# Sink attention and an erf-softplus feed-forward layer on one core: weight blocks held, converted and split two at a time

## The chip, the cores and the metric

The kernel runs on one core of a Trainium2 chip. The metric is the device time of one launch in microseconds (us). A profile of one execution comes with it. In the profile PE is TensorE (matmuls), PEld its weight loads, DVE VectorE, ACT ScalarE, POOL GpSimd, and SP the engine whose queue issues nearly all DMAs.

## The reference

Inputs are `q`, `k`, `v` of shape 4 x 8 x 768 x 64 (batch, heads, positions, head size), float32, and two weight matrices in float64: `w_in` 512 x 2048 and `w_out` 2048 x 512.

```python
keep = (pos[None, :] < n_sink) | ((rel >= 0) & (rel < window))      # n_sink 4, window 128
scores = where(keep, q @ k.T / sqrt(D), -1e9)
a = softmax(scores);  attn = a @ v                                   # -> x: 3072 tokens x 512
h = x @ w_in
g = h * erf(softplus(h))
out = g @ w_out                                                      # float32
```

## The kernel before

**Work.** Tokens are handled in 12 groups of 256. A group needs four attention steps (two heads each; `s` counts them over the whole kernel, 48 in all), and then 16 slices `f` of 128 hidden columns. `m` = 16 x group + f counts slices. Two slices share one PSUM tile `h`, of which there are two; `act` turns a tile into `g` with three ACT squares in a row, three more into a ring `u`, and three DVE passes (line 635), the first of which reads `h` and so frees its tile. `project` multiplies `g` by `w_out` and adds into `o`.

**Two kinds of product.** From group 1 on each float32 value is a pair of rounded parts, high and low, and a product takes three matmuls (lines 616 and 656 to 658). Group 0 uses the plain float32 weights `wf` (lines 612 and 653), since the pairs are not made yet. The profile counts each such float32 matmul twice.

**Weights.** There are 32 blocks of 128 x 512: 16 of `w_in`, 16 of `w_out`. `wload` brings a block in as raw 64-bit words (512 KB), `wconv` makes float32 of it on DVE in three passes (lines 513, 517, 523), the last few with an ACT copy behind (530), and `wsplit` makes the pair: an ACT cast for the high part (536), a DVE subtraction for the low part (537). Raw words, float32 blocks and pairs share one pool of 33 tiles of 4 KB a partition. The passes of `wconv` work in tiles of the ring `u`, which has three buffers and belongs to `act` as well.

**An attention step** is: `prep` (transposes of q and k on PE, a copy to `kq` on ACT), `score` (PE into `ps`; DVE masks at 343 and 348; ACT exponentials at 352), `norm` (DVE, for steps 4 to 7 ACT too), `ptrans` (PE transposes 383 and 384; ACT copies `pa` and `pz`; POOL selections at 397) and `av` (PE, line 424). `core(s)` is `av(s - 2)` followed by `score(s)`. `xh` and `xl` (442, 443) are the pair of a step's result; slice 0 of group 1 needs those of steps 4 to 7.

**Order.** Every engine works its own queue strictly in order. The order is not written by hand: each piece gets a priority from its step `a` = m + 10 and a table of offsets, and a scheduler that simulates the program places instructions by it. A change of sizes can therefore move instructions on every engine.

Of the kernel before, what the change touches and what calls it, by code (L numbers as in the profile page):

```python
# [19 lines left out]
P = 128  # L20
# [16 lines left out]
W1 = 7  # L37
WQ = 5
# [14 lines left out]
def kernel(  # L53
# [27 lines left out]
    wpool = ctx.enter_context(tc.tile_pool(name="wpool", bufs=33))  # L81
# [49 lines left out]
    def fast_path():  # L131
        with ExitStack() as st:
# [107 lines left out]
            def first_v():  # L240

                t = first_tile("v")
# [242 lines left out]
            staged = {}  # L485
# [3 lines left out]
            order = sorted(range(32), key=need)  # L489
            split = {}  # L490
            for n in range(32):
                split.setdefault(NF - 5 + n // 4 * 4 + n % 4 if n < 16 else NF + n - 16 + 1, []).append(n)

            def wload(n):

                src = wblock(n)
                t = staged[n] = wpool.tile([P, 2 * DM], I32, tag="wo", name=f"ws_{n}")
                if src.dtype == F32:
                    nc.sync.dma_start(t[:, :DM].bitcast(F32), src)
                else:  # L500
                    nc.sync.dma_start(t, src.bitcast(I32))

            def wconv(n, wn):

                s = staged.pop(n)
                if wblock(n).dtype == F32:
                    t = s[:, :512].bitcast(F32)
                else:
# [14 lines left out]
                    nc.vector.scalar_tensor_tensor(  # L523
                        out=ti if late else wf[n].bitcast(I32), in0=w[:, :, 0], scalar=29, in1=ti,
                        op0=ALU.logical_shift_right, op1=ALU.bitwise_or,
                    )
                    if not late:
                        return
# [282 lines left out]
```

## Time and profile before

| | us |
|---|---|
| median of 3 runs (763.35 to 765.52) | 763.46 |
| the profiled execution, as timed | 763.33 |
| span of its trace | 761.6 |
| PE busy / ACT / DVE / POOL | 720.0 / 549.0 / 494.2 / 231.9 |

The timed execution is 1.7 us longer than the span of its trace. A busy PE is not PE at its peak: its granted clock falls to half after pauses, and this is shown beside the stretches. The page's slices show PE below nine tenths only in roughly the first fifth of the span and at the very end.

### The profile page before, as it was taken

Reading aid. Unit: us, or ns where it says so; the run is one execution under the profiler, and the core shown is the slowest. Engines: PE = TensorE matmul, PEld = TensorE weight load, DVE = VectorE, ACT = ScalarE, POOL = GpSimd, SP = SyncE. Lnnn points to the kernel's source line nnn. Section 1 sums busy time; section 2 is a strip of 40 time slices with the busy share of each in tenths; the row PEclk is TensorE's granted clock in tenths of the full one; section 3 lists DMA queues with packets and bytes.
Section 4 is the critical chain, followed back from the end, with each engine's and each line's share of the span. In section 5 each row is a group of like instructions: output and inputs, shape, how many; then the busy total and the mean of one; then the engine's idle time right before and its main releaser. Section 6 shows DMA issues by size and latency. Waiting matters only on the chain. (4 is left out here: it accounts for less than half of the span.)

```text
span 761.6 us, 16545 instructions
## 1 busy us (share of the span) xinstructions
PE 720.0 (95%) x5840; PEld 612.9 (80%) x5840; DVE 494.2 (65%) x1383; ACT 549.0 (72%) x1293; POOL 231.9 (30%) x289
## 2 busy tenths in 40 slices
PE   4678998799999999999999999999999999999997
PEld 3456575688898898898898898888888888889895
DVE  5999977886565575576476475485476476475352
ACT  3446696987886786787687687687687687696574
POOL 0352211224224234233333333333332332332222
PEclk9688999999999999999999999999999999999999
DMA  8987512211311321221212222212222221110000
GB/s 229 234 273 262 166 36 49 75 32 34 85 44 35 83 51 32 71 46 42 72 43 50 77 45 44 64 41 52 60 49 53 53 63 43 43 46 2 28 2 32
DMA packets 115963, 54.13 MB, mean 71 GB/s; under 512 B 93153, under 2 KB 108513, under 8 KB 115873
## 3 DMA queue, kind: packets, MB, share of 16 engines
q1 hardware_dynamic: 114944, 52.86, 26.3%
q8 instruction: 49, 0.80, 0.5%
q14 instruction: 42, 0.34, 0.1%
q10 hardware_dynamic: 928, 0.13, 0.1%
HBM read 38.28 MB, written 6.29 MB: 59 GB/s over the span
## 5 line engine op out<-in xcount | busy, mean ns | idle before, releaser
L616 PE MATMUL h<-xh,wt 128*128 128x256 f32 x1408 | 273.5, 284 | 5.6 <-DVE acc L635 5.6
L616 PEld LDWEIGHTS h<-xh,wt 128*128 128x128 f32 x1408 | 224.4, 189 | 14.0 <-DVE acc L635 8.3
L616 PE MATMUL h<-xl,wt 128*128 128x256 f32 x704 | 198.4, 282 | 0.0
L641 POOL TENSOR_TENSOR g<-acc,g 128x512 fp32r<-128x512 f32 x88 | 114.1, 1297 | 272.8 <-DVE g L640 228.5
L633 ACT ACTIVATE u<-r 128x512 f32<-128x512 f32 x288 | 163.7, 622 | 14.7 <-DVE wf L523 7.1
L635 DVE SCALAR_TENSOR_TENSOR acc<-u,h 128x512 f32<-128x512 f32 x88 | 60.4, 686 | 140.1 <-POOL g L641 70.4
L656 PE MATMUL o<-wt,g 128*128 128x512 f32 x352 | 141.7, 402 | 0.0
L397 POOL TENSOR_SCALAR_AFFINE_SELECT pz<-pa 64x256 f32<-64x256 f32 x96 | 67.3, 701 | 243.0 <-ACT pa L387 239.9
L657 PE MATMUL o<-wt,g 128*128 128x512 f32 x352 | 139.4, 396 | 0.0
L616 PEld LDWEIGHTS h<-xl,wt 128*128 128x128 f32 x704 | 132.9, 189 | 4.6 <-issue 0.5
L635 DVE SCALAR_TENSOR_TENSOR acc<-u,acc 128x512 f32<-128x512 f32 x176 | 124.7, 709 | 17.8 <-DVE acc L635 0.9
L658 PE MATMUL o<-wt,g 128*128 128x512 f32 x352 | 135.4, 397 | 0.0
L352 ACT ACTIVATE pst<-pst,neg 128x144 f32<-128x144 f32 x192 | 77.4, 404 | 32.6 <-DVE neg L348 31.7
L658 PEld LDWEIGHTS o<-wt,g 128*128 128x128 f32 x352 | 65.8, 187 | 14.9 <-POOLq L779 0.5
L628 ACT ACTIVATE r<-h 128x512 f32<-128x512 f32 x96 | 56.9, 592 | 26.4 <-PE h L616 23.9
L657 PEld LDWEIGHTS o<-wt,g 128*128 128x128 f32 x352 | 66.1, 188 | 11.7
L656 PEld LDWEIGHTS o<-wt,g 128*128 128x128 f32 x352 | 66.1, 188 | 11.5 <-ACT ot L662 0.4
L630 ACT ACTIVATE r<-r 128x512 f32<-128x512 f32 x96 | 60.7, 632 | 2.7
L629 ACT ACTIVATE r<-r 128x512 f32<-128x512 f32 x96 | 60.9, 635 | 2.0
L442 ACT CAST xh<-av 128x256 fp32r<-128x256 f32 x44 | 16.0, 365 | 53.1 <-PE av L424 53.1
L367 DVE TENSOR_SCALAR pst<-pst,sum 128x128 f32<-128x128 f32 x176 | 50.5, 350 | 1.5
L286 ACT COPY kq<-tqk 128x512 f32<-128x512 f32 x48 | 28.0, 585 | 32.6 <-PE tqk L283 28.3
(86 smaller groups left out, 933.5 us busy)
## 6 DMA issues: line engine op xcount, KB each, us to landing
ws<-in_moe_w_in_dram SPq DMA_DIRECT2D x16, 512.0 KB, 5.1
ws<-in_moe_w_out_dram SPq DMA_DIRECT2D x16, 512.0 KB, 5.7
v<-in_v_dram SPq DMA_DIRECT2D x64, 96.0 KB, 2.3
out_dram<-ot SPq DMA_DIRECT2D x24, 256.0 KB, 2.1
q<-in_q_dram SPq DMA_DIRECT2D x88, 64.0 KB, 2.2
k<-in_k_dram SPq DMA_DIRECT2D x88, 64.0 KB, 2.1
vz<-v SPq DMA_DIRECT2D x88, 64.0 KB, 2.1
kq<-kq SPq DMA_DIRECT2D x32, 64.0 KB, 2.0
```

Of the source, the lines that this page charges most:

```text
L352: nc.scalar.activation(y, y, AF.Exp, bias=d["neg"][:, i, h : h + 1], scale=-1.0, accum_out=d["sum"][:, i, h : h + 1])
L397: nc.gpsimd.affine_select(out=out, in_=x, pattern=[[0, 2], [0, 2], [-sg, HP]], compare_op=op, fill=0.0, base=0, channel_multiplier=sg,)
L616: nc.tensor.matmul(o, wt[NC * j + c][:, p, fs], xt[e][:, c, :], start=(m == 0), stop=(m == len(ops) - 1))
L628: nc.scalar.activation(r, h, AF.Tanh, bias=b_t, scale=0.5)
L629: nc.scalar.activation(r, r, AF.Square, bias=b_v, scale=-0.5)
L630: nc.scalar.activation(r, r, AF.Square, bias=b_r)
L633: nc.scalar.activation(u, r, AF.Square, bias=b_a[i], scale=CS)
L635: nc.vector.scalar_tensor_tensor(out=acc, in0=u, scalar=CC[i] * CS**2, in1=x, op0=ALU.add, op1=ALU.mult)
L641: nc.gpsimd.tensor_tensor(gl, acc, gh.bitcast(F32), op=ALU.subtract)
L656: nc.tensor.matmul(o, gh[:, ws], wt[16 + f][:, 0, :], start=(f == 0), stop=False)
L657: nc.tensor.matmul(o, gh[:, ws], wt[16 + f][:, 1, :], start=False, stop=False)
L658: nc.tensor.matmul(o, gl[:, ws], wt[16 + f][:, 0, :], start=False, stop=(f == NF - 1))
```

## The change

Blocks go two to a tile. `wload` brings 1 MB in one DMA; `wconv` makes its three DVE passes over 1024 words, in place in the tile `wf`, with no ring `u` and no ACT copy; each conversion's first pass is told to follow the last pass of the conversion before. `wsplit` casts and subtracts 1024 words. High parts live in tiles of four blocks, in a ring of eight 8 KB tiles that the raw pairs use too; low parts and float32 pairs share 17 tiles of 4 KB. First `q`, `k` and `v` tiles lie in the ring of eight.

```diff
-WQ = 5
+WQ = 3
-    wpool = ctx.enter_context(tc.tile_pool(name="wpool", bufs=33))
+    wpool = ctx.enter_context(tc.tile_pool(name="wpool", bufs=17))
+    hpool = ctx.enter_context(tc.tile_pool(name="hpool", bufs=8))
...
-            order = sorted(range(32), key=need)
+            order = sorted(range(0, 32, 2), key=need)
...
-                t = staged[n] = wpool.tile([P, 2 * DM], I32, tag="wo", name=f"ws_{n}")
+                t = staged[n] = hpool.tile([P, 2, 2 * DM], I32, tag="big", name=f"ws_{n}")
...
-                    nc.sync.dma_start(t, src.bitcast(I32))
+                    nc.sync.dma_start(t, src.bitcast(I32).rearrange("(i p) d -> p i d", p=P))
...
-                    t = work.tile([P, 512], F32, tag="u", bufs=UB, name=f"w_{n}")
-                    w = s.rearrange("p (n t) -> p n t", t=2)
-                    ti = t.bitcast(I32)
...
-                    late = wn >= 33 - WQ
-                    if not late:
-                        wf[n] = wpool.tile([P, 2 * DM], F32, tag="wo", name=f"wf_{n}")[:, :DM]
...
-                wf[n] = wpool.tile([P, 2 * DM], F32, tag="wo", name=f"wf_{n}")[:, :DM]
-                nc.scalar.copy(wf[n], t)
+                d = wpool.tile([P, 2, DM], F32, tag="wf", name=f"wf_{n}")
+                w = s.rearrange("p i (n t) -> p (i n) t", t=2)
+                ti = d.rearrange("p i n -> p (i n)").bitcast(I32)
+                first = nc.vector.tensor_scalar(
+                    ti, w[:, :, 1], 0x07FFFFFF, 3, op0=ALU.bitwise_and, op1=ALU.logical_shift_left
+                )
+                follow(mark.get("c"), first)
...
+                mark["c"] = nc.vector.scalar_tensor_tensor(
+                    out=ti, in0=w[:, :, 0], scalar=29, in1=ti, op0=ALU.logical_shift_right, op1=ALU.bitwise_or
+                )
...
             def wsplit(n):
 
-                t = wf.pop(n)
-                d = wt[n] = wpool.tile([P, 2, DM], F32R, tag="wo", name=f"wt_{n}")
-                nc.scalar.copy(d[:, 0, :], t)
-                nc.vector.tensor_tensor(d[:, 1, :], t, d[:, 0, :].bitcast(F32), op=ALU.subtract)
+                d = wp.pop(n)
+                if n % 4 == 0:
+                    hq[n // 4] = hpool.tile([P, 4, DM], F32R, tag="big", name=f"wh_{n}")
+                hi_ = hq[n // 4][:, n % 4 : n % 4 + 2]
+                lo_ = wpool.tile([P, 2, DM], F32R, tag="wf", name=f"wl_{n}")
+                nc.scalar.copy(hi_, d)
+                nc.vector.tensor_tensor(lo_, d, hi_.bitcast(F32), op=ALU.subtract)
```

What the scheduler makes of it is seen in the order of instructions. Lines 612, 616, 635, 653 of before are 606, 610, 629, 647 of the change; 513, 517, 523 are 515, 520, 523; 536 and 537 are 535 and 536. In a name the first number is the step, slice or block, the last a running number.

Place 1, DVE, around the first pass of the first `act` (`gf_1`, slices 0 and 1). Before, from the conversion of blocks 10 and 11 on:

```order
L513 TENSOR_SCALAR w_11_686<-ws_11_606 128x512
L517 SCALAR_TENSOR_TENSOR w_10_679<-ws_10_599,w_10_679 128x512
L523 SCALAR_TENSOR_TENSOR wf_9_655<-ws_9_592,w_9_652 128x512
L517 SCALAR_TENSOR_TENSOR w_11_686<-ws_11_606,w_11_686 128x512
L523 SCALAR_TENSOR_TENSOR wf_10_682<-ws_10_599,w_10_679 128x512
L343 COPY_PREDICATED ps_5_617<-tri_134,ps_5_617 64x2x2x64
L523 SCALAR_TENSOR_TENSOR wf_11_689<-ws_11_606,w_11_686 128x512
L635 SCALAR_TENSOR_TENSOR gf_1_716<-u0_1_720,h_0_659 128x512
```

With the change the same pass stands here:

```order
L515 TENSOR_SCALAR wf_18_559<-ws_18_497 128x1024
L520 SCALAR_TENSOR_TENSOR wf_18_559<-ws_18_497,wf_18_559 128x1024
L523 SCALAR_TENSOR_TENSOR wf_18_559<-ws_18_497,wf_18_559 128x1024
L515 TENSOR_SCALAR wf_8_595<-ws_8_532 128x1024
L629 SCALAR_TENSOR_TENSOR gf_1_650<-u0_1_654,h_0_601 128x512
L520 SCALAR_TENSOR_TENSOR wf_8_595<-ws_8_532,wf_8_595 128x1024
```

Sixteen blocks are converted ahead of it before; with the change twelve, and the first pass of two more.

Place 2, DVE, the masks of attention step 7 (`ps_7`). Before, the first three splits of the kernel (`wt_0`, `wt_1`, `wt_2`) lie around them, and `gf_11` comes later:

```order
L537 TENSOR_TENSOR wt_0_1175<-wf_0_325,wt_0_1175 128x512
L443 TENSOR_TENSOR xl_1_845<-av_5_956,xh_1_844 128x256
L343 COPY_PREDICATED ps_7_973<-tri_134,ps_7_973 64x2x2x64
L635 SCALAR_TENSOR_TENSOR gf_9_1090<-u2_9_1100,gf_9_1090 128x512
L537 TENSOR_TENSOR wt_1_1201<-wf_1_332,wt_1_1201 128x512
L343 COPY_PREDICATED ps_7_973<-tri_134,ps_7_973 64x2x2x64
L348 ISA pst_142,neg_7_972<-ps_7_973,mask_84 128x144
```

With the change:

```order
L536 TENSOR_TENSOR wl_10_1472<-wf_10_621,wh_8_1373 128x1024
L629 SCALAR_TENSOR_TENSOR gf_15_1172<-u2_15_1182,gf_15_1172 128x512
L443 TENSOR_TENSOR xl_1_755<-av_5_842,xh_1_754 128x256
L536 TENSOR_TENSOR wl_20_1476<-wf_20_663,wh_20_1475 128x1024
L343 COPY_PREDICATED ps_7_859<-tri_137,ps_7_859 64x2x2x64
L536 TENSOR_TENSOR wl_12_1587<-wf_12_743,wh_12_1586 128x1024
L343 COPY_PREDICATED ps_7_859<-tri_137,ps_7_859 64x2x2x64
L536 TENSOR_TENSOR wl_22_1590<-wf_22_674,wh_20_1475 128x1024
L348 ISA pst_145,neg_7_858<-ps_7_859,mask_87 128x144
```

There are now eleven of the sixteen pair splits, and all eight `act` of group 0, ahead of the masks of step 7; the last five splits follow directly.

Place 3, PE, around `core(7)`, that is `av_5` and the scores of step 7. Before, it stands between the projection of `gf_7` and the hidden slices 12 and 13 of group 0:

```order
L653 MATMUL o_0_1_864<-wf_23_758,gf_7_1004 128x512
L424 MATMUL av_5_956<-pa_5_704,v_5_502 64x64 x2
L424 MATMUL av_5_956<-pa_5_704,v_5_502 64x128 x2
L424 MATMUL av_5_956<-pa_5_704,v_5_502 64x64 x2
L424 MATMUL av_5_956<-pz_5_705,vz_139 64x64 x8
L331 MATMUL ps_7_973<-kq_137 64x208 x2
L331 MATMUL ps_7_973<-kq_137 64x224 x2
L331 MATMUL ps_7_973<-kq_137 64x208 x2
L331 MATMUL ps_7_973<-kq_137 64x224 x2
L283 MATMUL tqk_8_1045<-ident_61,k_8_998 128x128 x2
L283 MATMUL tqk_8_1045<-ident_61,q_8_995 128x128 x2
L612 MATMUL h_12_1178<-xf_0_424,wf_12_828 128x256
```

With the change:

```order
L647 MATMUL o_0_1_774<-wf_28_903,gf_13_1097 128x512
L424 MATMUL av_5_842<-pa_5_638,v_5_484 64x64 x2
L424 MATMUL av_5_842<-pa_5_638,v_5_484 64x128 x2
L424 MATMUL av_5_842<-pa_5_638,v_5_484 64x64 x2
L424 MATMUL av_5_842<-pz_5_639,vz_142 64x64 x8
L331 MATMUL ps_7_859<-kq_140 64x208 x2
L331 MATMUL ps_7_859<-kq_140 64x224 x2
L331 MATMUL ps_7_859<-kq_140 64x208 x2
L331 MATMUL ps_7_859<-kq_140 64x224 x2
L283 MATMUL tqk_8_923<-ident_64,k_8_884 128x128 x2
```

Group 0 has done all its hidden slices and seven of its eight projections by then. What follows is one projection, nine matmuls of group 1, and the transposes of step 7.

## Rows read from the trace of the kernel before

**Rows 1.** Busy time of each engine in stretches of the span (us from its start), each with its number of instructions; then the granted PE clock as a share of full speed, the DMA share and GB/s.

```profile
20.00:30.00 10.00, 5.22 (x37) 4.42 (x37) 9.80 (x41) 4.79 (x18) 2.15 (x4) 0.55 0.88 176
50.00:60.00 10.00, 4.47 (x35) 3.21 (x34) 8.77 (x17) 4.99 (x10) 5.62 (x4) 0.93 0.92 315
60.00:70.00 10.00, 10.00 (x28) 6.86 (x29) 9.94 (x28) 6.30 (x18) 0.00 (x0) 0.73 0.99 367
90.00:100.00 10.00, 10.00 (x78) 6.89 (x77) 9.80 (x18) 8.43 (x17) 3.74 (x4) 1.00 0.12 29
120.00:130.00 10.00, 7.19 (x57) 4.93 (x59) 6.21 (x23) 6.59 (x18) 2.04 (x4) 0.84 0.18 40
140.00:150.00 10.00, 7.49 (x48) 6.92 (x47) 8.77 (x25) 9.91 (x25) 2.02 (x2) 0.87 0.39 105
200.00:300.00 100.00, 99.61 (x859) 87.75 (x858) 63.45 (x185) 78.06 (x185) 33.38 (x43) 1.00 0.23 57
```

**Rows 2.** PE in order of time: start, duration, line, operation, out<-in, count, and in brackets the idle time before with what ended it.

```profile
59.95 6.37 PE L612 MATMUL h<-xf,wf 128*128 128x256 f32 x16 [5.53 <-DVE gf L635]
...
70.14 3.62 PE L612 MATMUL h<-xf,wf 128*128 128x256 f32 x16
...
127.00 1.12 PE L424 MATMUL av<-pa,v 128*64 128x64 f32 x12 [2.81 <-issue]
...
143.67 0.39 PE L656 MATMUL o<-wt,g 128*128 128x512 f32 x1
143.90 0.40 PE L657 MATMUL o<-wt,g 128*128 128x512 f32 x1
146.81 0.39 PE L616 MATMUL h<-xh,wt 128*128 128x256 f32 x1 [2.51 <-DVE acc L635]
...
156.05 0.28 PE L616 MATMUL h<-xh,wt 128*128 128x256 f32 x1
156.17 0.28 PE L616 MATMUL h<-xl,wt 128*128 128x256 f32 x1
```

**Rows 3.** DVE in order of time, the same columns: the wait for a raw block and the first `act`; neighbours of 512 and 256 elements that do not depend on each other; then four passes of which the second and third read what the one before them wrote; then the first instruction behind the masks of step 7.

```profile
55.11 0.43 DVE L513 TENSOR_SCALAR w<-ws 128x512 int32<-128x512 int32 x1 [1.17 <-DMA ws<-in_moe_w_in_dram]
...
59.13 0.67 DVE L635 SCALAR_TENSOR_TENSOR gf<-u,h 128x512 f32<-128x512 f32 x1
...
74.28 0.68 DVE L523 SCALAR_TENSOR_TENSOR wf<-ws,w 128x512 int32<-128x512 int32 x1
74.88 0.42 DVE L513 TENSOR_SCALAR w<-ws 128x512 int32<-128x512 int32 x1
75.22 0.69 DVE L523 SCALAR_TENSOR_TENSOR wf<-ws,w 128x512 int32<-128x512 int32 x1
75.83 0.41 DVE L443 TENSOR_TENSOR xl<-av,xh 128x256 fp32r<-128x256 f32 x1
76.16 0.69 DVE L517 SCALAR_TENSOR_TENSOR w<-ws,w 128x512 int32<-128x512 int32 x1
...
94.16 0.44 DVE L513 TENSOR_SCALAR w<-ws 128x512 int32<-128x512 int32 x1
94.63 0.78 DVE L517 SCALAR_TENSOR_TENSOR w<-ws,w 128x512 int32<-128x512 int32 x1
95.45 0.78 DVE L523 SCALAR_TENSOR_TENSOR w<-ws,w 128x512 int32<-128x512 int32 x1
96.15 0.67 DVE L635 SCALAR_TENSOR_TENSOR gf<-u,h 128x512 f32<-128x512 f32 x1
...
101.63 0.69 DVE L537 TENSOR_TENSOR wt<-wf,wt 128x512 fp32r<-128x512 f32 x1
```

**Rows 4.** ACT in order of time, the same columns: the first `act` and its wait for a buffer of the ring `u`; one late copy; neighbours of 256 and of 512 elements.

```profile
50.68 0.60 ACT L628 ACTIVATE r<-h 128x512 f32<-128x512 f32 x1 [1.51 <-PE h L612]
...
57.05 0.63 ACT L633 ACTIVATE u<-r 128x512 f32<-128x512 f32 x1 [3.78 <-DVE wf L523]
...
92.89 0.62 ACT L530 COPY wf<-w 128x512 f32<-128x512 f32 x1
...
97.31 0.37 ACT L442 CAST xh<-av 128x256 fp32r<-128x256 f32 x1
97.57 0.63 ACT L633 ACTIVATE u<-r 128x512 f32<-128x512 f32 x1
98.26 0.62 ACT L536 CAST wt<-wf 128x512 fp32r<-128x512 f32 x1
98.78 0.59 ACT L628 ACTIVATE r<-h 128x512 f32<-128x512 f32 x1
```

**Rows 5.** One attention step, number 9, followed over three engines: scores on PE, both masks on DVE (with one split between), normalisation on DVE, transposes on PE, the copy `pa` on ACT, then `av_8` and the scores of step 10 on PE.

```profile
128.91 1.62 PE L331 MATMUL ps<-kq 64*64 64x208 f32 x16
...
130.66 0.90 DVE L343 COPY_PREDICATED ps<-tri,ps 64x256 f32<-64x256 int8 x2
...
132.31 0.31 DVE L348 CUSTOM_DVE_ANT_0 pst<-ps,mask 128x144 f32<-128x144 f32 x1
...
135.47 0.87 DVE L367 TENSOR_SCALAR pst<-pst,sum 128x128 f32<-128x128 f32 x4
...
135.90 0.89 PE L383 MATMUL tp<-ident,pst 128*128 128x128 f32 x4 [1.25 <-DVE pst L367]
...
136.88 0.59 ACT L387 COPY pa<-tp 128x512 f32<-128x512 f32 x1 [0.16 <-PE tp L383]
...
137.61 0.67 PE L424 MATMUL av<-pa,v 128*64 128x64 f32 x12 [0.62 <-ACT pa L387]
138.68 0.99 PE L331 MATMUL ps<-kq 64*64 64x208 f32 x16
```

More of the change, by code (lines that the diff above doesn't have):

```diff
@@ L482, in attn @@
                         fn(s)
-            staged = {}
+            staged, wp, hq = {}, {}, {}
             def need(n):
                 return 4 * (n // 4) if n < 16 else n - 16 + LAG
-            order = sorted(range(32), key=need)
+            order = sorted(range(0, 32, 2), key=need)
             split = {}
-            for n in range(32):
-                split.setdefault(NF - 5 + n // 4 * 4 + n % 4 if n < 16 else NF + n - 16 + 1, []).append(n)
+            for n in range(0, 32, 2):
+                split.setdefault(NF - 5 + n if n < 16 else NF + n - 16 + 1, []).append(n)
@@ new lines, in wconv @@
+                for i in range(2):
+                    wf[n + i] = d[:, i, :]
+                if w_in.dtype == F32:
+                    nc.vector.tensor_copy(d, s[:, :, :DM].bitcast(F32))
+                    return
+                w = s.rearrange("p i (n t) -> p (i n) t", t=2)
[3 more added lines that the diff above has]
+                )
@@ new lines, in wconv @@
+                follow(mark["t", 2] if wn < 2 else mark["t", 3] if wn < 4 else mark["s", 3], first)
+                follow(mark.get("c"), first)
+                nc.vector.scalar_tensor_tensor(
+                    out=ti, in0=w[:, :, 1], scalar=-0x40000000, in1=ti, op0=ALU.bitwise_and, op1=ALU.bitwise_or
+                )
+                mark["c"] = nc.vector.scalar_tensor_tensor(
+                    out=ti, in0=w[:, :, 0], scalar=29, in1=ti, op0=ALU.logical_shift_right, op1=ALU.bitwise_or
+                )
@@ new lines, in wconv @@
+                wp[n] = d
+            def wsplit(n):
+                d = wp.pop(n)
[5 more added lines that the diff above has]
+                nc.vector.tensor_tensor(lo_, d, hi_.bitcast(F32), op=ALU.subtract)
+                for i in range(2):
+                    wt[n + i] = (hi_[:, i], lo_[:, i])
@@ L550, in fast_path @@
                 first_sinks()
-                for n in order[:2]:
-                    wload(n)
+                wload(order[0])
             with at(0, "load"):
                 vf = first_v()
-                for n in order[2:WQ]:
+                for n in order[1:WQ]:
                     wload(n)
@@ L586, in fast_path @@
                             gs[m // 2] = mlp.act(hp, m, g == 0)
[L588 removed]
+                while wn < 16 and a >= 2 and (2 * wn < (2, 4, 4)[a - 2] if a < 5 else wn < a - 2 or need(order[wn]) <= m + W1):
                     with at(a, "wc"):
[L590 removed]
+                        wconv(order[wn], 2 * wn)
                     wn += 1
[L592 removed]
+                    if wn + WQ <= 16:
                         with at(a, "wl"):
```

52 lines of the change are left out of this document (14 added, 38 removed).

## The prediction

> **What bounds the kernel now.** I read the busy times by stretch first [rows 1]. From 200 us on PE is busy 99.6% at full clock, while DVE and ACT have a quarter or more free: what the change does there is hidden behind PE. Before that it is otherwise. DVE is busy 9.8 to 10 of 10 us from 20 to 100 (8.8 in the stretch with a DMA wait), and PE loses time and, after pauses, half its clock (0.55, 0.73, 0.84, 0.87). The kernel gets shorter only if PE reaches its closed stretch sooner.
>
> Second, PE in order of time, for its pauses [rows 2]. The largest: 5.53 us, ended at 59.95 by the first pass of the first `act`; the eight matmuls behind it (16 entries) take 6.37 where the same at full clock take 3.62, so the pause costs another 2.75. Then 2.81 before `av_7` at 127.00, and 2.51 before slice 20 at 146.81. From 156 on there is nothing left to win.
>
> Third, why the first `act` is late. Its `h` is ready at 50.68, but its `u` waits 3.78 us for a buffer that a conversion holds [rows 4]; in DVE's queue it stands behind sixteen converted blocks, one of which waited 1.17 us for its DMA, and it starts at 59.13 [rows 3].
>
> **The change part by part.**
>
> *DVE price.* What counts in a saturated queue is the distance from start to start: 0.60 us for a two-input pass of 512, 0.33 to 0.34 for the first pass of 512 and for a two-input pass of 256 [rows 3]. So a two-input pass has 0.07 fixed and 0.53 for each 512: 1024 take 1.13. The first pass moves at twice the rate: 0.60 for 1024. A pair costs 0.60 + 1.13 + 1.13 = 2.87 instead of 2 x 1.54 = 3.07, and its split 1.13 instead of 1.20: 16 x 0.27 = 4.3 us saved. Against it stands that passes of one block, back to back, lie further apart: 0.47 and 0.82 instead of 0.34 and 0.60 [rows 3], 0.36 a pair. Before, two or three blocks alternate; the change chains them in place. At worst all 16 pairs pay: 5.8 us, so the bounds on DVE are -4.3 and +1.5. In the new order most passes have something between them after the first `act`, so I take the free spacing there. The skill puts the fixed part on DVE at about 60 ns and advises grouping when the engine is saturated (Trainium skill, Perfetto Trace Analysis, Optimizing Scalar/DVE Operations); the trace agrees with 0.07.
>
> *ACT price.* 0.26 from start to start for 256 elements, 0.52 for 512 [rows 4]: nothing fixed to see, a cast of 1024 takes 1.03, and pairing saves nothing. The same section gives ACT 93 ns for operands in SBUF, which would save an estimated 16 x 0.093 = 1.5 us; the sum does without it. Four late copies of 0.62 go: 2.5 us.
>
> *Ring `u` and loads.* Conversions leave the ring, so `u` can follow `h` at once: 50.68 plus three squares of about 0.63 is 52.6, and the first pass can start at 53.3. Loads are half as many and twice as large; three pairs instead of five blocks start early, half a MB more in front of the next keys, 1.6 us at the 315 GB/s of [rows 1]. I price it at nothing, since `av_0` and its followers wait for POOL there; without that cover it costs those 1.6 us. The 1.17 us wait should go, since the seventh pair's load now stands far ahead in SP's queue.
>
> *The first `act`.* By place 1, four blocks less stand in front of it, 6.1 us of DVE, less 0.60 for one new pass. From 59.13 less 1.17 that makes 52.5, so `u` at 53.3 decides. PE needs the tile at about 54.4 (59.95 less 5.53). The pause of 5.53 and the 2.75 of half clock disappear: **PE starts group 0 some 8 us earlier.**
>
> *What stands behind it now.* This is the term that decides. DVE's new order from `gf_1` to the masks of step 7 (place 2) holds: the last two passes of a pair (2.27) and nine whole pairs (25.8), 24 `act` passes at 0.60 (14.4), **eleven pair splits** at 1.13 (12.4), masks and sums of steps 5 and 6 (2.3 each: masks 0.92 twice, the rest small passes), masks of step 7 (1.8), two `xl` (0.7): 62.0 us. From 53.3 that ends at 115.3, with 2.3 us of waits for ACT's sixteen casts and eight `act` (which fill ACT as well) at about **117.6. Before, these masks ended at 101.6** [rows 3]. The splits were held back before by the full pool of 33 tiles; now they run ahead of step 7, and on PE `core(7)` stands behind seven projections (place 3). So the lead of 8 us is paid back: `gf_15` is done at about 112, its projection, the last of group 0, 3.5 us later, and group 1 can't go on without steps 6 and 7.
>
> *From there*, by [rows 5]: exponentials, sums and the normalisation with two splits of 1.13 between them take 4.7, transposes and `pa` another 0.6: `av_6` at 122.9. PE has paused for 5 us, so `av` and scores take the half-clock 3.5 us that they took from 127.00 to 130.5 [rows 2, 5]: scores of step 8 end at 126.4. A step without splits between: masks 1.9, exponentials 0.6, norm 1.3, copy and hops 1.3, so `av_7` at 131.5, against 127.00. Scores of step 9 end at 135.0, slices 16 and 17 run to 139 at 0.12 a matmul [rows 2], ACT's squares for them hold `pa_9` to 141.4, and the scores of step 10 end at 143.6 (139.7 before, [rows 5]). From here on the change is ahead again: all splits are done, so the wait of 2.51 at 146.81 and the half clock behind it don't come. 24 matmuls (2.8), twelve projection matmuls at 0.23 (2.8), 24 more (2.8), nine projection matmuls (2.1), transposes (0.6), and 0.3 of gaps bring PE to 155.0, where before it stands at 156.05 [rows 2].
>
> *Sum:* 156.05 - 155.0 = 1.0 us gained; behind it PE is closed in both. 763.33 (the profiled execution, 0.13 below the median) - 1.0 = **762.3 us**. The instruments here tell a change from none at about 0.3%, 2.3 us, so the forecast is no difference to be measured.
>
> **The rivals.**
>
> 1. *No change beyond 0.3%*, as worked out: 761.2 to 765.7. For it: both the lead (8.3) and the repayment come from sums of many rows. Chance 0.38.
>
> 2. *Faster: the lead stays.* If the masks of step 7 end by about 112 rather than 117.6, because the splits find their casts unfinished and are few by then, or PE reaches `core(7)` sooner, `av_7` comes at 126 and the ramp of group 1 still has its free DVE: 762.3 less 5 to 6, **757**. It decides from masks ending at 115. For it: by PE's work alone, two hidden tiles and three projections move ahead of `core(7)`, five pieces of about 3.6 [rows 2], 18 us less the lead of 8: masks at 101.6 + 10 = 111.6. Against it: DVE's 62.0 us of work leave it no choice, if the passes cost what I take. Chance 0.33.
>
> 3. *Slower: step 7 waits still longer.* If most of the nine pairs before the masks pay 0.36 for following themselves, DVE is 3.2 us later, and the longer pause of PE costs a second half-clock stretch like that of [rows 2], 2.75: 762.3 + 6, **768**. It decides from masks ending at 119. For it: the chain in place; DVE has no slack. Against it: an `act` pass stands between most passes. Length alone could do it too: masks or sums that come ready behind a pass of 1.13 instead of 0.60 wait up to 0.53 longer, at some ten places in steps 5 to 8, 5.3 us at most, 767.6. The same section of the skill has that rule: where an engine makes bubbles on others, breaking up instructions lets work finish sooner; no run here shows it yet. Chance for all of this 0.29.
>
> That the change does not do what it says (the ring wait stays) would leave the start at 59 and all splits at their new place; it is in the third.
>
> The range takes the middles of both rivals and about a fifth left out: 756.5 to 769. Forecast alone: 760.5 to 765.5. Faster by over 0.3%: 0.33; within: 0.38; slower: 0.29.
>
> **What the next profile would show.** Right: the first `act` on DVE at 53 to 54 with no conversion wait ahead of ACT's `u`; no PE pause before slice 4 and no 0.73 clock at 60 to 70; DVE busy without a break to about 118; masks of step 7 ending at 116 to 119; PE idle for 8 us or more in all between 110 and 140, at half clock in part; splits finished by 125; no pause before slice 20. A pass of 1024 at 1.13 and a first pass at 0.60 from start to start. Wrong: a first pass of 1024 at 1.13 (no double rate) would add 16 x 0.53 = 8.5 us to DVE; a wait for a raw pair on DVE after 35 us would mean that loads, not DVE, set the pace; a PE below 99% after 160 us would mean that a new order costs something in the closed stretch, which I price at nothing because DVE and ACT have a quarter free there [rows 1].

## The result: slower by 1.2%, and the profile after

| | before | after |
|---|---|---|
| median, us | 763.85 (763.35 to 765.52) | 773.39 (771.31 to 774.48) |
| profiled execution, us; its span | 763.33; 761.6 | 773.8; 772.1 |
| first `act` pass starts on DVE | 59.13 [rows 3] | 62.15 |
| masks of step 7 end on DVE | 101.7 [rows 3] | 128.3 |

The ratio is 1.0118 (95% interval 1.0091 to 1.0145), some 9.5 us. The forecast was 762.3 with a range to 769.0; both missed. Stretches of the profile after, with the columns of [rows 1]:

```profile
20.00:30.00 10.00, 2.85 (x28) 2.29 (x28) 8.07 (x28) 2.92 (x11) 3.81 (x4) 0.54 1.05 298
50.00:60.00 10.00, 7.39 (x46) 6.61 (x47) 6.13 (x6) 2.01 (x4) 4.16 (x6) 0.66 0.77 273
120.00:130.00 10.00, 6.44 (x45) 3.70 (x39) 9.88 (x20) 2.66 (x10) 0.26 (x1) 1.00 0.29 66
200.00:300.00 100.00, 99.21 (x858) 87.25 (x858) 62.02 (x181) 77.61 (x184) 31.16 (x40) 1.00 0.23 57
```

Behind 200 us next to nothing has changed: 99.21 against 99.61. The loss lies before, and it begins earlier than any term of the forecast. From 20 to 30 us PE is busy 2.85 where it was 5.22 [rows 1], and DVE, which I had called saturated, 8.07 against 9.80. The first long wait is on ACT, for the copy of the next keys; PE's transposes wait for ACT, and DVE for them (three engines, in order of time):

```profile
32.58 0.59 ACT L286 COPY kq<-tqk 128x512 f32<-128x512 f32 x1 [7.29 <-DMA kq<-kq]
...
33.21 1.12 PE L383 MATMUL tp<-ident,pst 128*128 128x128 f32 x4 [4.02 <-ACT kq L286]
...
33.73 0.31 DVE L348 CUSTOM_DVE_ANT_0 pst<-ps,mask 128x144 f32<-128x144 f32 x1 [5.42 <-PE tp L383]
```

That DMA is the second `kq<-kq` copy in the queue of SP, which tells why it is late:

```profile
22.17 0.51 SPq L130 DMA_DIRECT2D kq<-kq  x1
22.72 0.60 SPq L251 DMA_DIRECT2D vz<-v_first  x1
23.37 0.59 SPq L502 DMA_DIRECT2D ws<-in_moe_w_in_dram  x1
24.00 0.68 SPq L502 DMA_DIRECT2D ws<-in_moe_w_out_dram  x1
24.80 0.48 SPq L130 DMA_DIRECT2D kq<-kq  x1
```

Two raw pairs of 1 MB stand in front of it. Over the first 50 us these copies take 4.1, 6.8 and 7.7 us (least, median, most) from issue to landing, the one behind the two pairs 7.7; before they took 2.7, 4.9 and 5.6.

On GpSimd the selects, two halves for each attention step, have grown as well. Steps 0 and 3 after, and the last pair of step 4, beside which DVE is idle:

```profile
23.38 1.24 POOL L397 TENSOR_SCALAR_AFFINE_SELECT pz<-pa 64x256 f32<-64x256 f32 x2 [21.08 <-ACT pa L387]
24.68 2.71 POOL L397 TENSOR_SCALAR_AFFINE_SELECT pa<-pa 64x256 f32<-64x256 f32 x2
...
47.92 1.94 POOL L397 TENSOR_SCALAR_AFFINE_SELECT pz<-pa 64x256 f32<-64x256 f32 x2 [3.50 <-ACT pa L387]
49.92 2.63 POOL L397 TENSOR_SCALAR_AFFINE_SELECT pa<-pa 64x256 f32<-64x256 f32 x2
...
57.99 0.90 POOL L397 TENSOR_SCALAR_AFFINE_SELECT pa<-pa 64x256 f32<-64x256 f32 x2
```

The second halves of the same steps in the kernel before, and PE's row behind the last of them:

```profile
24.51 1.30 POOL L397 TENSOR_SCALAR_AFFINE_SELECT pa<-pa 64x256 f32<-64x256 f32 x2
...
43.43 1.37 POOL L397 TENSOR_SCALAR_AFFINE_SELECT pa<-pa 64x256 f32<-64x256 f32 x2
...
44.86 0.91 PE L424 MATMUL av<-pa,v_first 128*64 128x128 f32 x8 [1.18 <-POOL pa L397]
```

2.71 against 1.30, 2.63 against 1.37. `av_3` on PE, which needs the last of these selects, starts at 52.61; before it started at 44.86. So the first `act`, which stands behind it on PE, is not earlier but 3.0 us later (PE, ACT and DVE; the last row is the last mask of step 7):

```profile
52.61 0.91 PE L424 MATMUL av<-pa,v_first 128*64 128x128 f32 x8 [3.98 <-POOL pa L397]
...
59.54 0.60 ACT L622 ACTIVATE r<-h 128x512 f32<-128x512 f32 x1 [2.58 <-PE h L606]
61.49 1.67 ACT L627 ACTIVATE u<-r 128x512 f32<-128x512 f32 x3
...
62.15 0.69 DVE L629 SCALAR_TENSOR_TENSOR gf<-u,h 128x512 f32<-128x512 f32 x1 [5.92 <-ACT u L627]
...
128.03 0.30 DVE L348 CUSTOM_DVE_ANT_0 pst<-ps,mask 128x144 f32<-128x144 f32 x1
```

ACT's `u` no longer waits for a buffer of the ring (3.78 in [rows 4]): its passes follow the squares directly. The change did there what it says, and it did not matter, because `r` reads its `h` at 59.54 instead of 50.68 [rows 4].

### The profile page after: what moved, and what is told of

The parts are those of the page before. It is cut to its first block, busy times and chain, and to the rows that moved or that the text cites. A ratio compares the mean times of both kernels' runs of the same rounds, so it can differ in the third digit from the quotient of the medians.

```text
span 772.1 us, 16428 instructions
## 1 busy us (share of the span) xinstructions
PE 721.6 (93%) x5840; PEld 613.2 (79%) x5840; DVE 487.2 (63%) x1319; ACT 545.3 (71%) x1273; POOL 228.0 (30%) x289
## 4 chain that ended last, share of the span: by engine, by line
PE 86%; DVE 6%; ACT 3%; DMA 2%; POOL 1%; issue 1%; ACTq 0%; SPq 0%; DVEq 0%
PE h L610 32%; PE o L650 11%; PE o L652 11%; PE o L651 11%; PE av L424 7%; PE ps L331 5%; PE tqk L283 3%; PE tp L383 3%; PE o L647 2%; PE h L606 2%; DMA kq<-kq 1%; DVE gf L629 1%; ACT pst L352 1%; DVE wl L536 1%; DVE ps L343 1%
## 5 line engine op out<-in xcount | busy, mean ns | idle before, releaser
L610 PE MATMUL h<-xh,wh 128*128 128x256 f32 x704 | 197.9, 284 | 3.5 <-DVE acc L629 3.5
L610 PE MATMUL h<-xl,wh 128*128 128x256 f32 x704 | 197.5, 281 | 0.0
L610 PE MATMUL h<-xh,wl 128*128 128x256 f32 x704 | 197.3, 281 | 0.0
L650 PE MATMUL o<-wh,g 128*128 128x512 f32 x352 | 141.9, 403 | 0.0
L610 PEld LDWEIGHTS h<-xh,wh 128*128 128x128 f32 x704 | 131.8, 188 | 10.9 <-DVE acc L629 6.0
L651 PE MATMUL o<-wl,g 128*128 128x512 f32 x352 | 139.3, 396 | 0.0
L610 PEld LDWEIGHTS h<-xl,wh 128*128 128x128 f32 x704 | 132.2, 188 | 4.4 <-issue 0.2
L652 PE MATMUL o<-wh,g 128*128 128x512 f32 x352 | 135.2, 396 | 0.0
L610 PEld LDWEIGHTS h<-xh,wl 128*128 128x128 f32 x704 | 132.2, 188 | 0.6 <-issue 0.2
L652 PEld LDWEIGHTS o<-wh,g 128*128 128x128 f32 x352 | 66.0, 188 | 14.8
L651 PEld LDWEIGHTS o<-wl,g 128*128 128x128 f32 x352 | 66.2, 188 | 11.7
L650 PEld LDWEIGHTS o<-wh,g 128*128 128x128 f32 x352 | 66.1, 188 | 11.4 <-ACT ot L656 0.4
```

The lines of the kernel that those rows point to most:

```text
L610: nc.tensor.matmul(o, wt[NC * j + c][p][:, fs], xt[e][:, c, :], start=(m == 0), stop=(m == len(ops) - 1))
L650: nc.tensor.matmul(o, gh[:, ws], wt[16 + f][0], start=(f == 0), stop=False)
L651: nc.tensor.matmul(o, gh[:, ws], wt[16 + f][1], start=False, stop=False)
L652: nc.tensor.matmul(o, gl[:, ws], wt[16 + f][0], start=False, stop=(f == NF - 1))
```

## Experiments

In the table, times are us in each run's own trace: the start of `av_3` on PE, of the first `act` pass on DVE, and the end of the masks of steps 5, 7 and 10 on DVE. Ratios are to the kernel before on the same chip, with 95% intervals; the kernel before had medians from 763.62 to 764.72 in these comparisons. A gain of 2 to 3 us over the change (e1, e4) is at the edge of what this tells: the intervals overlap with that of the change. The execution of e5 that was profiled took 773.63, the other four 769.21 to 770.42, so the times in its row are not those of its median.

| kernel | `av_3` | first `act` | masks 5 | masks 7 | masks 10 | median | ratio |
|---|---|---|---|---|---|---|---|
| before | 44.86 | 59.13 | 62.4 | 101.7 | 146.1 | 763.85 | |
| after | 52.61 | 62.15 | 70.7 | 128.3 | 157.7 | 773.39 | 1.0118 |
| e1 | 50.61 | 60.03 | 68.6 | 124.9 | 158.6 | 770.96 | 1.0094 (1.0072 to 1.0116) |
| e2 | 53.16 | 62.63 | 71.2 | 127.5 | 162.3 | 774.40 | 1.0125 (1.0099 to 1.0151) |
| e3 | 47.19 | 59.30 | 62.6 | 100.6 | 146.4 | 764.61 | 1.0010 (0.9999 to 1.0022) |
| e5 | 51.46 | 61.20 | 67.9 | 113.3 | 157.8 | 769.37 | 1.0065 (1.0040 to 1.0091) |
| e16 | 45.10 | 53.64 | 60.3 | 115.6 | 154.0 | 765.28 | 1.0013 (0.9998 to 1.0028) |
| e4 | 53.60 | 62.87 | 71.4 | 120.1 | 155.5 | 770.74 | 1.0083 (1.0061 to 1.0104) |
| e6 | 50.76 | 60.15 | 68.7 | 117.1 | 157.5 | 769.08 | 1.0056 (1.0042 to 1.0070) |
| e7 | 44.11 | 52.34 | 59.0 | 112.5 | 149.0 | 765.52 | 1.0008 (0.9990 to 1.0025) |
| e8 | 43.29 | 54.97 | 69.2 | 119.1 | 158.6 | 771.32 | 1.0088 (1.0061 to 1.0115) |
| e10 | 44.02 | 53.80 | 62.5 | 100.1 | 139.1 | **752.59** | 0.9844 (0.9816 to 0.9871) |
| e17 | 44.84 | 58.89 | 61.8 | 100.0 | 146.0 | 764.41 | 1.0007 (0.9990 to 1.0025) |

### The early slip

**Keys first.** From after: the key copies of steps 0 and 1 keep their order on SP and go ahead of the raw pairs.

```
-                dcopy(kq[:, c, 0, :P], kq[:, c, 2, :P])
+                mark["kc"] = follow(mark.get("kc"), dcopy(kq[:, c, 0, :P], kq[:, c, 2, :P]))
+                if s == 0:
+                    mark["kc0"] = mark["kc"]
...
-                    nc.sync.dma_start(t, src.bitcast(I32).rearrange("(i p) d -> p i d", p=P))
+                    follow(mark.get("kc0"), nc.sync.dma_start(t, src.bitcast(I32).rearrange("(i p) d -> p i d", p=P)))
```

> The changed kernel, but on SP's queue the key copies of steps 0 and 1 (in order 0, 1) stand ahead of the raw weights from ws_6 on, which were ahead of the copy of step 0. Theory A (the key copy of step 0 went out at 24.80 behind ws_6 and ws_16 and landed 7.7 us later; ScalarE's copy of kq for step 4 waited 7.3 us for it, and the first act came 8.9 us later than forecast): the copy goes out near 24 us with no load right ahead of it and lands some 5 us later, as it did before the change; the wait falls from 7.3 to 3 to 5 us, the first gf comes at 58 to 60 instead of 62.15, and the time is 768.5 to 771. Theory B (what sets the time is the eleven splits ahead of the masks of step 7, and the early slip only moves idle time): the wait shortens, the time stays at 772.5 to 774.5.

PE's early rows came about 2 us earlier (`av_3` 50.61 against 52.61) and the median fell by 2.4 us: a part, not the whole. The first select of step 1 comes 3.5 us earlier (32.00 against 35.52), but 1.5 of this are lost again by `av_3`, mostly between `av_1` and the selects of step 2, where PE runs at half clock (3.6 us, in the change 2.4).

**Keys by GpSimd.** From after: for s < 4 the copy is `nc.gpsimd.tensor_copy` instead of a DMA.

> The changed kernel, but the key copies of steps 0 to 3 are made by GpSimd instead of a transfer on SP's queue, so nothing on that queue stands ahead of them. Theory A: ScalarE's copy of kq for step 4 comes at 25.3 to 26.5 instead of 32.58, TensorE's transposes of step 1 at about 27.5 instead of 33.21, the first gf at 54 to 56 instead of 62.15, and the time is 764 to 767. Theory B: the early rows move so, but the time stays within 1.5 us of 773.4.

No gain. The wait that it was aimed at went (ACT's copy, first row), but the next small transfer, `vz`, now stood behind the raw load and took its place (ACT, PE and SP of this run):

```profile
26.81 0.59 ACT L289 COPY kq<-tqk 128x512 f32<-128x512 f32 x1 [1.33 <-PE tqk L286]
...
31.18 1.12 PE L427 MATMUL av<-pz,vz 128*64 128x64 f32 x16 [2.63 <-DMA vz<-v_first]
...
22.90 0.38 SPq L505 DMA_DIRECT2D ws<-in_moe_w_in_dram  x1
23.32 0.52 SPq L251 DMA_DIRECT2D vz<-v_first  x1
```

**The bytes alone.** From before: `WQ = 6`, six blocks instead of five early, the same half MB more as in the change.

> The kernel before with six raw blocks loaded early instead of five: the same 3 MB ahead of the next keys as in the changed kernel, but both key copies of steps 0 and 1 still stand ahead of the later loads. If the half MB more is by itself the cause of the late key copy (A1): the wait for the key copy grows from 0.86 to 4 us or more and the time to 768 or more. If the cause is that two loads of 1 MB pass the key copy (A2): the keys of step 4 land about 1.2 us later (PE's transposes at 25.1 instead of 23.96), and the time is 763.5 to 765.5. Theory B expects no change at all, 763.4 to 764.3.

1.001, no difference that can be told in the time. The early rows do move: ACT's copy of the next keys waits 3.05 us for its DMA (0.86 before), the first select of step 1 starts at 32.15 (30.52 before), and `av_3` at 47.19 (44.86). What hides it is that `u` waits for the ring here anyway, 2.33 us instead of 3.78 [rows 4]:

```profile
57.83 0.63 ACT L633 ACTIVATE u<-r 128x512 f32<-128x512 f32 x1 [2.33 <-DVE wf L523]
```

The change has no such wait, so this run does not show that the half MB costs nothing there. That the place of the small copies costs beside the bytes is shown by e1, which has the same bytes in front and starts step 1's selects 3.5 us earlier than the change.

**Short passes.** From after: the three passes of a pair run on each half, 512 words at a time; all else stays.

```
+                for i in range(2):
+                    w = s[:, i].rearrange("p (n t) -> p n t", t=2)
+                    ti = d[:, i].bitcast(I32)
...
```

> The changed kernel with its conversions done 512 words at a time (six passes for a pair instead of three), everything else kept: pairs, rings, loads, order of the splits. Theory C: GpSimd's selects of the attention steps are held up while VectorE is inside a long pass (the four selects of step 3 took 4.6 us in the changed kernel and 2.3 us before, of step 0 3.9 and 2.3 us; with VectorE idle 1.8 us), and so the first act slips. Then the selects of step 0 and step 3 take 2.3 to 3.2 us again, the row av of step 3 comes 1.5 to 3 us earlier than 52.61, and since VectorE pays some 0.2 us per pair more (2 x 0.60 for 1.13, 2 x 0.33 for 0.60), 2 to 3 us over the pairs, the time is 770.5 to 773. Rival D: the selects vary by themselves; the rows of av stay, and the time rises by the passes, 774.5 to 777.

A gain of 4.0 us in the median, a little more than expected. In the trace, that of the long execution, `av_3` is only 1.2 us earlier: ACT's key copy waits still longer there, 7.94 us. The second selects of steps 0 and 3 in this run:

```profile
25.26 1.57 POOL L397 TENSOR_SCALAR_AFFINE_SELECT pa<-pa 64x256 f32<-64x256 f32 x2
...
49.83 1.57 POOL L397 TENSOR_SCALAR_AFFINE_SELECT pa<-pa 64x256 f32<-64x256 f32 x2
```

2.71 and 2.63 became 1.57 and 1.57. The selects are the same instructions on the same data; what changed is the length of the passes beside them on DVE.

Length is not all of it. Where DVE runs pass behind pass with hardly a gap, selects grow beside passes of 512 too, in the kernel before at step 4 and in e8 (below) at step 5:

```profile
49.23 5.47 POOL L397 TENSOR_SCALAR_AFFINE_SELECT pz<-pa 64x256 f32<-64x256 f32 x2 [4.43 <-ACT pa L387]
```

```profile
80.99 11.20 POOL L397 TENSOR_SCALAR_AFFINE_SELECT pz<-pa 64x256 f32<-64x256 f32 x2 [22.95 <-ACT pa L387]
```

There PE had projections and hidden slices to do meanwhile; in steps 0 to 3 it has little else, and `av` waits for the selects.

**Both, without any hold.** From after: the first edit above, and halves for the first seven pairs alone.

> The changed kernel with the early slip undone and no hold on the order: key copies of steps 0 and 1 ahead of the raw weights from ws_6 on, first seven pairs converted 512 words at a time. First gf at 52 to 54 instead of 62.15. If the slip reaches the end one to one: 764 to 765.5, as e7, whose splits were held too. If the splits ahead of the masks of step 7 add their own loss (e4 gained 2.7 us): 766 to 769.

This takes back 8.1 of the 9.5 us; 0.6 us are left against the kernel before in its own comparison (764.72), no difference that can be told. The first `act` starts where the forecast had it (53.3):

```profile
53.64 0.69 DVE L633 SCALAR_TENSOR_TENSOR gf<-u,h 128x512 f32<-128x512 f32 x1 [1.12 <-ACT u L631]
```

Since e16 is e1 with shorter early passes and nothing else, the two also give the price of the length: 5.7 us of the medians, and 5.5 us of `av_3`. The first rows of `av_1` in e1 and in e16:

```profile
35.78 0.91 PE L426 MATMUL av<-pa,v_first 128*64 128x128 f32 x8 [2.35 <-POOL pa L399]
```

```profile
35.03 0.55 PE L426 MATMUL av<-pa,v_first 128*64 128x128 f32 x8 [1.24 <-POOL pa L399]
```

From the first select of step 1 to `av_3` e1 takes 18.61 us and e16 13.36. Of the 5.25 between them 2.85 are the selects of steps 1 to 3 themselves, and 2.40 are what stands between these: PE, which waits longer for the selects in e1, does the same `av` and transposes there at half clock (granted clock during `av_1` 0.50 in e1, 1.00 in e16).

The build orders the rest anew, so some of the 8.1 may be order: five splits stand ahead of the masks of step 7 here, eleven in the change.

### The order behind the first `act`

**Splits behind step 7.** From after: the subtraction of each split follows the masks of step 7.

```
-                nc.vector.tensor_tensor(lo_, d, hi_.bitcast(F32), op=ALU.subtract)
+                follow(mark["t", 7], nc.vector.tensor_tensor(lo_, d, hi_.bitcast(F32), op=ALU.subtract))
```

> The changed kernel, but VectorE's subtractions of the splits stand behind the masks of step 7 (eleven stood ahead of them, 1.13 us each). Theory A alone: the first gf stays at 62.15, the masks of step 7 end at 114 to 117 instead of 128.26, and the time falls little, to 771 to 773, since the same work has to be done before the weights of group 1 are ready. Theory B: the attention steps 7 to 9 all come some 10 us earlier, TensorE's idle stretch from 120 to 150 us (10.4 us idle and half the clock from 130 on) closes, and the time falls to 763 to 767.

Masks 7 came 8.2 us earlier, the time fell by 2.7: the same splits then stand ahead of steps 8 and 9.

**It adds to the first.** Both edits together (e6), then with the first seven pairs in halves (e7).

> The changed kernel with the edits of the runs e1 (key copies ahead of the raw weights) and e4 (splits behind the masks of step 7) together. They gained 2.4 and 2.7 us. If the one moves the whole chain earlier and the other shortens it later, they add: 767.5 to 769.2. If both only fill the same idle time of TensorE between 120 and 150 us: 770 to 771.5.

> The changed kernel with the edits of e1 and e4 and with the first seven pairs converted 512 words at a time, the rest 1024. Theory C: selects of steps 0 and 3 back to 2.3 to 3.2 us, the first gf 2 to 4 us earlier than in e1 (60.03), the time 765 to 767.5. Rival D: as e6, or up to 1.5 us slower.

e6 gained 4.3 where its parts gave 2.4 and 2.7; the halves of e7 gained 3.6 more. e7 is level with the kernel before, and no better than e16, which lacks the hold: once the slip is gone, holding splits is worth nothing more.

**The kernel before, conversions in place.** From before: all three passes of a block write its own `wf`, so they leave the ring `u` (but for the last four blocks, which keep it and their ACT copy); widths, loads and the common pool of 33 stay. The main line of the edit:

```
-                    t = work.tile([P, 512], F32, tag="u", bufs=UB, name=f"w_{n}")
+                    t = wf[n] = wpool.tile([P, 2 * DM], F32, tag="wo", name=f"wf_{n}")[:, :DM]
...
```

> The kernel before with one part of the change alone: the passes of a conversion write the block's own tile instead of a tile of the u ring (512 words, single blocks, one ring of weights, loads as before). By step 4 of the prediction the pause of ScalarE for the ring (3.78 us) goes and the first act comes 4 to 6 us earlier. If what is gained there reaches the end: 758 to 760.5. If the masks of step 7 or the weights of group 1 are late anyway (the lead is spent): 762.5 to 765.

This is one part of the change alone, without long passes and large loads, and it is 7.4 us slower, outside both of the expected ranges. Its first `act` is 4.2 us earlier than before, and its masks 7 are 17.4 us later. From the end of masks 4 to that of masks 6 DVE converts 74 passes (39 and 35) here, 55 (29 and 26) in the kernel before. The wait for a ring buffer had been holding conversions behind the masks.

**The same, with the order held.** e8, and late blocks wait for the masks of a step.

```
-                    follow(mark["t", 2] if wn < 2 else mark["t", 3] if wn < 4 else mark["s", 3], first)
+                    follow(mark["t", 2] if wn < 2 else mark["t", 3] if wn < 4 else mark["s", 3]
+                           if wn < 16 else mark["t", 5] if wn < 25 else mark["t", 6], first)
```

> Run e8 (the kernel before with conversions in their own tiles, 771.3 us) with the conversions held to the order that the kernel before had: blocks 16 to 24 behind the masks of step 5, later ones behind those of step 6; no work is taken away. Theory E: masks of step 5, 6, 7 come at 57 to 61, 77 to 81 and 97 to 101 instead of 69.2, 97.0 and 119.1, and the time is 759 to 764. Rival F (the amount of VectorE's work and the early first act decide, not the order): 769 to 772.

752.59, 11.9 us under the kernel before in the same comparison, faster than both kernels of this study, and better than either range. First `act` and the last mask of step 7, in e8 and in e10:

```profile
54.97 0.67 DVE L636 SCALAR_TENSOR_TENSOR gf<-u,h 128x512 f32<-128x512 f32 x1
...
118.82 0.30 DVE L348 CUSTOM_DVE_ANT_0 pst<-ps,mask 128x144 f32<-128x144 f32 x1
```

```profile
53.80 0.67 DVE L636 SCALAR_TENSOR_TENSOR gf<-u,h 128x512 f32<-128x512 f32 x1
...
99.75 0.30 DVE L348 CUSTOM_DVE_ANT_0 pst<-ps,mask 128x144 f32<-128x144 f32 x1
```

And PE around the ramp and after it, before, e8 and e10 (columns of [rows 1]):

```profile
44.00:70.00 26.00, 19.61 (x101) 14.91 (x102) 24.71 (x56) 14.12 (x34) 7.14 (x5) 0.79 0.90 321
120.00:160.00 40.00, 32.53 (x282) 26.76 (x281) 30.28 (x83) 34.40 (x82) 11.45 (x15) 0.91 0.22 54
160.00:740.00 580.00, 576.86 (x4868) 507.42 (x4867) 352.16 (x1001) 433.02 (x1009) 184.95 (x230) 1.00 0.20 48
```

```profile
44.00:70.00 26.00, 23.44 (x101) 16.69 (x95) 25.88 (x58) 15.31 (x35) 2.41 (x4) 0.80 0.97 335
120.00:160.00 40.00, 28.75 (x255) 24.21 (x255) 28.20 (x77) 31.61 (x80) 7.95 (x13) 0.79 0.24 59
```

```profile
44.00:70.00 26.00, 24.43 (x119) 17.89 (x120) 25.87 (x60) 17.72 (x39) 4.63 (x4) 0.87 0.85 286
120.00:160.00 40.00, 36.06 (x318) 30.14 (x317) 33.07 (x92) 36.18 (x91) 12.89 (x18) 0.96 0.30 69
160.00:740.00 580.00, 580.00 (x4898) 511.26 (x4897) 342.61 (x993) 444.23 (x1010) 184.70 (x230) 1.00 0.20 48
```

Both win PE time from 44 to 70. From 120 to 160 e8 gives it back (28.75 against 32.53), e10 gains again (36.06). Behind 160 us e10 has no pause left; before had eight, 3.1 us in all, each of some 0.4 where an `h` waits for DVE (why they are gone in e10 was not followed):

```profile
PE h L616 <- DVE acc L635: 3.1, 8, 0.4
```

**The holds alone.** From before: the holds of e10, nothing else.

> The kernel before with the holds of run e10 alone (blocks 16 to 24 behind the masks of step 5, later ones behind step 6); the u ring stays. If the gain of e10 comes from the early first act kept by the order: no change, 762 to 766, first gf near 59. If the holds alone would have brought it: 752 to 757.

Nothing. The ring already kept that order; the hold is worth something only where the ring is gone.

### What did not reach the fastest one

Six kernels sought e10's gain in the change by holds like its own. e9: splits spread behind the masks of steps 7 to 11; e11: e9 and late pairs behind masks 5 and 6; e13: e11 and `gf` passes of slices 8 to 15 behind masks 6 and 7; e14: e13 and e1.

> The changed kernel with its splits spread as the one ring of weights spread them before: the subtraction for block group j of the first weights stands behind the masks of step 7 + j, of the second weights behind the masks of step 8 + j, so two to five splits between two steps. Theory E (what costs is the order on VectorE: without the u ring and the common ring nothing paces conversions and splits, and they stand ahead of the masks of steps 5 to 9, whose steps feed group 1): masks of step 7 at 120 as in run e4, of step 10 at 149 to 152 instead of 157.7 (e4: 155.5), time 766.5 to 769. Rival F (the work of VectorE up to the first act of group 1 counts, not its order): the splits are needed by then anyway, time as e4, 770 to 772.

> The changed kernel with splits as in run e9 and its conversions held back: pairs from the ninth behind the masks of step 5, from the thirteenth behind those of step 6. The early slip (first gf at 62.15) stays. Theory E: masks of step 6 at 92 to 95 instead of 99.9, of step 7 at 112 to 117, of step 10 at 145 to 149; time 764.5 to 767.5. Rival F: 770 to 773.

> Run e11 (changed kernel, conversions and splits held) with the activation passes held as well: those of slices 8 and 9 behind the masks of step 6, from slices 10 and 11 on behind those of step 7. The early slip stays. If the order is the rest: masks of step 6 at 89 to 92 (e11: 93.5), of step 7 at 105 to 109 (111.8), time 763 to 767. If the pairs cost by themselves: masks 7 earlier, time 768 to 770.

> Run e13 with the key copies of steps 0 and 1 ahead of the raw weights (as e1, which gained 2.4 us): first gf at 59 to 60.5; if the order is the rest, 760.5 to 764.5, some 2.5 us under e13; if the pairs cost by themselves 766 to 768.

Measured: 771.20 (ratio 1.0086, 1.0054 to 1.0117), 768.99 (1.0063, 1.0043 to 1.0084), 770.79 (1.0090, 1.0073 to 1.0107) and 766.51 (1.0042, 1.0017 to 1.0066). Masks 7 came at 121.1, 111.8, 111.2 and 107.8. None reached the range of its theory of the order. e9 and e14 lie in the range of the rival (the work, or the pairs by themselves, cost), e11 and e13 in neither. Then, with the slip taken out as in e16: e12 with e11's holds, e15 with e13's.

> Run e11 and the two edits against the early slip (key copies ahead of the raw weights as in e1, first seven pairs 512 words at a time as in e7). Theory A + E (both the early slip and the order cost, and nothing else does): first gf at 52 to 54, masks of step 7 at 103 to 109, of step 10 at 139 to 144; time 757 to 762, faster than the kernel before. If the slip and the order only share one loss: as e7, 764 to 766.

> Run e12 with the activation passes held as in e13: slip undone (first seven pairs 512 words at a time), and the order of the masks as in e10. If the order is the rest: first gf at 52.5 to 54, masks of step 7 at 101 to 106, of step 10 at 139 to 144, time 754 to 760. If the pairs cost by themselves: 762 to 765, as e12.

764.61 (1.0010, 0.9992 to 1.0027) and 762.25 (0.9983, 0.9966 to 1.0000): both miss the range of the order and lie in that of the rival (e12: slip and order share one loss; e15: the pairs cost by themselves). They are 12 and 10 us above e10, though the first `act` comes at 52.97 and 53.84. About 3.5 us of that lie behind 180 us (PE busy 556.53 of 560 in e15, 560.00 in e10). The rest lies before: masks 7 at 104.1 and masks 10 at 149.2 in e15, 100.1 and 139.1 in e10. So the order that made e10 fast is not enough in the change. Whether the pairs, the ring of high parts or the rest of the order keeps it there was not settled; no run made the change with single blocks.

## Why the prediction was wrong, step by step

**DVE price: right.** DVE after, in order of time:

```profile
82.20 1.23 DVE L520 SCALAR_TENSOR_TENSOR wf<-ws,wf 128x1024 int32<-128x1024 int32 x1
83.34 0.69 DVE L629 SCALAR_TENSOR_TENSOR gf<-u,gf 128x512 f32<-128x512 f32 x1
...
85.08 0.70 DVE L515 TENSOR_SCALAR wf<-ws 128x1024 int32<-128x1024 int32 x1
85.68 0.69 DVE L629 SCALAR_TENSOR_TENSOR gf<-u,gf 128x512 f32<-128x512 f32 x1
86.28 1.23 DVE L520 SCALAR_TENSOR_TENSOR wf<-ws,wf 128x1024 int32<-128x1024 int32 x1
87.54 1.32 DVE L523 SCALAR_TENSOR_TENSOR wf<-ws,wf 128x1024 int32<-128x1024 int32 x1
```

From start to start a two-input pass takes 1.14 (forecast 1.13), the first pass 0.60 (0.60), and a pass whose successor reads it 1.26. The 8.5 us named as a danger did not come.

**ACT price: misread, small.** The prediction saw no fixed part, from a cast of 256 that reads PSUM and rows of 512 that read SBUF, and put a cast of 1024 at 1.03. After, two of them and what follows:

```profile
77.31 2.00 ACT L535 CAST wh<-wf 128x1024 fp32r<-128x1024 f32 x2
79.21 0.62 ACT L623 ACTIVATE r<-r 128x512 f32<-128x512 f32 x1
```

That is 0.95 each, against 2 x 0.52 for two of 512 [rows 4]: some 1.4 us saved on ACT over sixteen pairs, near the 1.5 that the prediction named and left out of its sum.

**Ring `u`: right; loads: a step that failed.** "I price it at nothing, since `av_0` and its followers wait for POOL there; without that cover it costs those 1.6 us." The cover did not hold: POOL waits for ACT, ACT for the key copy (7.29). The 1.6 us are about what the bytes alone do to step 1 (e3: 32.15 against 30.52), but they are not all: a 64 KB copy behind two loads of 1 MB lands 7.7 us after its issue, and the first select of step 1 starts 5.0 us later than before (35.52). Of the 7.75 us that `av_3` is late, 2.0 come back when the copies go first (e1). The working looked at SP's queue for the seventh pair's load alone, not for the small copies that now stand between the pairs.

**A term left out, by the medians the larger one.** Nothing in the sum priced what longer DVE passes do to GpSimd, and through it to PE. Another 5.5 of the 7.75 us come back when the early passes are shortened as well (e16 against e1); in the median this length is worth 4.0 us alone (e5) and 5.7 behind e1, the place of the copies 2.4 (e1). Step 0's selects took 3.95 us (1.24 + 2.71) after, 2.27 (0.97 + 1.30) before. Rival 3 had "length alone" as its second half, but applied it to masks and sums on DVE, at most 5.3 us; here it was another engine whose own instruction grew. Masks and sums that wait have no part in the 5.25 us between e1 and e16. What the Trainium skill says there of breaking up instructions (Perfetto Trace Analysis, Optimizing Scalar/DVE Operations) it says of an engine that is not saturated; DVE was busy for 18.2 of the 22.6 us from 30.0 to 52.6, and shorter passes gained all the same. In steps 0 to 3 a half took at most 2.71 after, and at most 1.58 before, 1.57 in e5 and 1.77 in e16. The Trainium skill has the rule (SBUF — State Buffer, SBUF: two separate sides): VectorE and GpSimd share a pair of ports as a lock held for a whole instruction, which a VectorE operation with two SBUF inputs takes against a GpSimd instruction that reads SBUF. The traces agree as far as they go: 0.90 with DVE idle, more beside passes of 1024 than beside 512 (2.71 against 1.57 in e5), most beside passes without gaps (11.20 in e8). That it is this lock and nothing else, no run here shows.

**The first `act`: 53.3 forecast, 62.15 measured.** Without the two causes above (e16) it is 53.64.

**From there to masks 7: size nearly right, start wrong.** Forecast 62.0 of work and 2.3 of waits, 64.3; measured 128.3 - 62.15 = 66.1. DVE is busy for 63.6 of it and idle for 2.6. Of the 10.7 by which 128.3 exceeds 117.6, 8.9 are the start and 1.8 this term.

**The tail: right in the change.** From masks 7 to `av_7` the forecast has 13.9 us (117.6 to 131.5), the change takes 14.6:

```profile
142.91 1.12 PE L424 MATMUL av<-pa,v 128*64 128x64 f32 x12 [0.61 <-ACT pa L387]
```

Masks 7 come 26.7 us later than the 101.6 of before and the span ends 10.5 later, so 16.2 us are won back behind them; the forecast had 17.0. The profiled execution is 11.5 us over the forecast (773.8 against 762.3): 8.9 the start, 1.8 the work up to masks 7, 0.8 the tail. With another order the tail does not hold. In e16 masks 7 end at 115.6, 2.0 before the forecast, yet `av_7` starts at 134.09 instead of 131.5 less 2.0: I had "a step without splits between" for step 8, and there nine splits stand between the masks of steps 7 and 8, and PE waits for that normalisation:

```profile
132.18 1.09 PE L385 MATMUL tp<-ident,pst 128*128 128x128 f32 x4 [7.62 <-DVE pst L369]
```

**The repayment: right in kind.** That a lead won by freeing the ring is paid back behind masks 7 is what e8 shows, at more than its full price. Rival 2, the lead that stays, is what e10 shows for the kernel before; in the change the same holds did not bring it (e15, 762.25). Rival 3 came nearest (slower, 768) with a price 5 us too small, and its nearness is luck: its own reasons, passes that pay 0.36 for following themselves and masks that wait, are not what the traces show to have made the first `act` late.

**The closed stretch: right.** Behind 180 us PE is busy 556.46 of 560 after, 556.86 before. That its eight short pauses could be won (e10) I had not seen: "From 156 on there is nothing left to win" was wrong by 3.1 us.

## What to carry to other kernels

A ring of buffers that makes an engine wait may be what holds back work that is not yet needed: when you free it, say which queue grows next, and hold that order by a dependence of its own. Before making transfers or passes longer, list the small transfers that share their queue and the engines that work beside them: both paid here, and the sum had the first at nothing and the second not at all. A cover ("it waits for POOL anyway") holds only if the covering engine is itself not waiting for what you move.

## What the runs showed of the hardware

- A half of GpSimd's selects (two instructions) took 0.90 with VectorE idle, 2.71 beside passes of 1024 words and 11.20 beside passes of 512 without gaps, with no wait in the profile: the instructions themselves grow.
- A copy of 64 KB on a queue behind two transfers of 1 MB took 7.7 us to land; the same copies took 4.9 in the median before.
- The same eight matmuls of `av` took 0.91 us at a granted clock of 0.50 (e1) and 0.55 at 1.00 (e16).
